# Slot counts of 544, 576 and 600 for the eight experts, and a token's slot computed by bit operations

## The chip, the cores and the metric

The kernel runs on one core of a Trainium2 chip. The metric is the device time of one execution in microseconds (us). The core has a matrix engine (TensorE, PE), a vector engine (VectorE, DVE), a scalar engine (ScalarE, ACT), a general engine (GpSimd, POOL) and a queue engine (SyncE, SP), which run side by side and wait for one another through semaphores. Data moves between the memory of the chip and the on-chip buffers through DMA queues that SP and POOL feed.

## The reference

An attention block feeds a routed two-layer network. Attention has 8 batches, 8 heads, 576 positions and a head width of 64. Scores below the row's maximum less `tau` are dropped before the softmax. The result, rearranged to 4608 tokens of 512 numbers, goes through one of 8 experts, which the token's id alone selects:

```python
expert_idx = token_ids * np.int64(2654435761) % np.int64(E)
out = np.zeros((N, D), dtype=np.float32)
for e in range(E):
    mask = expert_idx == e
    ...
    h = np.maximum(xe @ w1[e], 0.0)      # 512 -> 1024
    out[mask] = h @ w2[e]                # 1024 -> 512
```

All of it is in 32-bit floats. The ids are part of the input; with the reference's inputs the experts get, sorted, 533, 565, 570, 571, 576, 596, 598 and 599 tokens.

## The kernel before, in words

**Attention.** The work is cut into 32 pairs `p` of heads (four pairs of heads, each over eight batches), and each pair into five steps, so that the loop over `n` has 160 steps and a few more to drain. In a step PE forms scores (`score`, L238), DVE negates them and finds the maximum (`negate`, L249), POOL adds the threshold (`thr`, L256), ACT takes the exponential (L263), DVE applies the mask one step later (`mask`, L274), PE turns the weights (L285) and multiplies them with v (L316). Once per pair POOL prepares the denominators (`rec`, L346) and scales the next keys (`scale_k`, L218), and DVE normalises (`put_xm`, L355); SP stores the result to `x_scratch`. The order is written out by hand; each engine works through its instructions in that order.

**Routing.** `route()` (L369 on) is a generator; the attention loop takes one piece of it about twice a pair. It counts the tokens per expert, sorts the experts by count (`pos` is an expert's place in that order, place 0 having the fewest), and gives each token a slot number. Place `e` has `caps[e]` slots for tokens; a token whose rank among its expert's tokens is beyond that goes to overflow tiles, which a loop at the end of the kernel works off (`For_i`, L1138). The table of slots has 608 entries per place, laid out as 32 rows `c` of 19 entries `s`. Entry (c, s) is the token in column 32 s + c of the place's tile: `s` counts squares of 32 columns, `c` the position in a square. With 18 full squares, rank r lies in row r // 18; the kernel computes that by a multiplication with 3641 and a shift, after subtracting what rows of 19 entries hold (`FULL`). After the slot is known (`slot_i`, L526), `scatters()` writes each token's number into one of two tables, one indirect DMA on POOL per step for 36 steps (L551); then SP reads the tables back (L562, L566), and DVE forms the indices for the early gathers (L571, L573).

**Experts.** They are taken by place. Place 0 is started inside the last attention steps: its tokens' rows are gathered by POOL in quarters as the heads finish (`fetch_0`, L122; the last quarter at L831), turned by PE (`early_xT`, L623), and multiplied with three quarters of w1 in `early_h` (L649), pieces of which `fill` puts among the last attention steps; `late_h` (L667) adds the last quarter and takes the ReLU. For the other places both layers are done with seven products of half-size blocks (`seven`, L945) instead of eight, at the cost of block sums on DVE (`sums_w1`, `sums_w2`, `sums_x`, `sums_h`, L862 and L865). The second layer of place 0 is done that way too. A block's width in columns is half of `caps[e]`.

While PE works on the second layer of place `e`, DVE turns the gathered rows of place e + 1 (`turn_x`, L1059), SP moves them into `xT` by sixteen transfers (L1067), and POOL gathers the rows of place e + 2 (`fetch`, L122). For place 1 the gathers start in `late_h`, each behind a small copy (`mark`, L1052) that reads a part of the hidden layer. The output of a place is turned by DVE in two parts (`put_squares`, L1031), and POOL scatters one square of 32 tokens per indirect DMA (L1039). The weights come by SP (L137, L143).

The functions that the diff touches and what calls them, with the profile's line numbers:

Of the kernel before, what the change touches and what calls it, by code (L numbers as in the profile page):

```python
# [9 lines left out]
FP32 = mybir.dt.float32  # L10
# [4 lines left out]
ALU = mybir.AluOpType  # L15
# [5 lines left out]
def kernel(  # L21
# [35 lines left out]
    KT, NB = 5, 19  # L57
    SL = 32 * NB
    CUT = 8
    CAP = SL - CUT  # L60
    FULL = NB * (32 - CUT)
    N_LOW = 5
    LOW = SL - 32
    caps = [LOW] * N_LOW + [CAP] * (E - N_LOW)
# [10 lines left out]
    assert all((r * 3641) >> 16 == r // (NB - 1) for r in range(N))  # L75
# [20 lines left out]
    slot_i = consts.tile([P, NTC], I32, name="slot_i")  # L96
# [50 lines left out]
    with tc.tile_pool(name="a_q", bufs=1) as a_q, \  # L147
# [221 lines left out]
        def route():  # L369
# [10 lines left out]
            cnt = rt_sb.tile([P, 2 * E], FP32, name="cnt")  # L380
# [9 lines left out]
            big = rt_sb.tile([P, NTC], FP32, name="big")  # L390
# [3 lines left out]
            big_e = rt_sb.tile([P, E], FP32, name="big_e")  # L394
# [21 lines left out]
            for e in (0, E // 2):  # L416
# [6 lines left out]
                if e == 0:  # L423
# [22 lines left out]
            nc.gpsimd.tensor_scalar(out=big_e[:], in0=pos[:], scalar1=float(N_LOW),  # L446
                                    scalar2=None, op0=ALU.is_ge)
# [5 lines left out]
                                    op=ALU.mult)  # L453
            yield
            nc.vector.scalar_tensor_tensor(out=key[:], in0=big_e[:], scalar=float(LOW - CAP),
                                           in1=cnt[:, E:2 * E], op0=ALU.mult, op1=ALU.add)
# [3 lines left out]
            nc.vector.tensor_scalar(out=ot_i[:], in0=key[:], scalar1=float(P - 1 - LOW),  # L460
# [14 lines left out]
            nc.vector.scalar_tensor_tensor(out=base[:], in0=pos[:], scalar=float(1 << 19),  # L475
                                           in1=base[:], op0=ALU.mult, op1=ALU.add)
# [14 lines left out]
            nc.vector.tensor_scalar(out=rank_i[:, 2], in0=rank_i[:, 0], scalar1=13, scalar2=63,  # L491
                                    op0=ALU.logical_shift_right, op1=ALU.bitwise_and)
            nc.vector.tensor_scalar(out=rank_i[:, 3], in0=rank_i[:, 0], scalar1=19, scalar2=None,
                                    op0=ALU.logical_shift_right)
            nc.gpsimd.tensor_copy(rank[:], rank_i[:, 1])
            nc.gpsimd.tensor_copy(place[:], rank_i[:, 3])
            nc.gpsimd.tensor_scalar(out=big[:], in0=place[:], scalar1=float(N_LOW),
                                    scalar2=None, op0=ALU.is_ge)
            nc.gpsimd.tensor_copy(ovt[:], rank_i[:, 2])
# [19 lines left out]
            yield  # L519
            nc.gpsimd.tensor_tensor(out=ovt[:], in0=ovt[:], in1=first[:], op=ALU.subtract)  # L520
            yield
            nc.vector.scalar_tensor_tensor(out=ovt[:], in0=rank_f[:], scalar=float(LOW),
                                           in1=ovt[:], op0=ALU.is_gt, op1=ALU.mult)
            nc.gpsimd.tensor_tensor(out=first[:], in0=first[:], in1=rank[:], op=ALU.add)
            yield
            nc.vector.scalar_tensor_tensor(out=slot_i[:], in0=first[:], scalar=-1.0, in1=ovt[:],  # L526
                                           op0=ALU.add, op1=ALU.add)
# [308 lines left out]
    with tc.tile_pool(name="m_x", bufs=1) as m_x, \  # L836
# [4 lines left out]
        NH = LOW // 64  # L841
# [4 lines left out]
        o_q = [m_x.tile([P, n, 32, CO], FP32, name=f"o_q{i}") for i, n in enumerate((NH, NB - NH))]  # L846
# [181 lines left out]
        def put_squares(e, i):  # L1028

            s0, s1 = ((0, NH), (NH, -(-caps[e] // 32)))[i]  # L1030
            nc.vector.transpose(  # L1031
                out=o_q[i][:, 0:s1 - s0].rearrange("p n a c -> p c n a"),
                in_=oT[:, :, 32 * s0:32 * s1].rearrange("p c (n q) -> p c n q", q=32))
# [48 lines left out]
        with tc.manual_schedule():  # L1082
            for e in range(E):
                more = e + 1 < E
# [117 lines left out]
```

## Time and profile before

| | |
|---|---|
| median of 3 runs | 922.66 us (922.28 to 922.70) |
| profiled execution, its own time | 933.93 us |
| its span, first to last instruction | 932.2 us, 20728 instructions |
| TensorE busy | 911.4 us, 98% |
| VectorE busy | 759.5 us, 81% |
| ScalarE busy | 458.3 us, 49% |
| GpSimd busy | 408.1 us, 44% |
| granted TensorE clock | 0.998 |
| DMA | 113.11 MB, mean 121 GB/s |

The profile is that of one execution. Busy shares are averages over stages with different limits, so the tables by stretches and the timeline of a seam say more than the page's first part. A group line gives line, engine, operation, output from input, shapes and count, then the busy time and the mean duration, then the idle time before it and who ended it. "issue" is time in which an engine waited for nothing that the profile shows. Ends of matmuls are modelled, so a PE that is shown busy may still be waiting a little.

### The profile page before, as it was taken

The page shows a single profiled execution, that of the slowest core. Times are in us where ns is not written, and L with a number is a line of the kernel's source. Part 1 is how long each engine was busy: PE and PEld are TensorE (multiplying, and loading weights), DVE is VectorE, ACT ScalarE, POOL GpSimd, SP SyncE. Part 2 cuts the span into 40 slices and gives each one's busy share as a digit, 9 for nine tenths or more (in the row PEclk, how much of TensorE's full clock was granted, in tenths as well). Part 3 has the DMA queues.
Part 4 walks back from the last instruction along what each step waited for, and adds up shares of the span by engine and source line. Part 5 has one row for each costly group of instructions (what it writes and reads, how often), then busy time and mean ns, then how long its engine had stood idle before and what let it go on. Part 6 is the DMA issues. An engine that isn't in the chain of part 4 may idle for free.

```text
span 932.2 us, 20728 instructions
## 1 busy us (share of the span) xinstructions
PE 911.4 (98%) x7495; PEld 662.9 (71%) x7495; DVE 759.5 (81%) x1658; ACT 458.3 (49%) x741; POOL 408.1 (44%) x522
## 2 busy tenths in 40 slices
PE   7999999999999999999999998999999999999996
PEld 4666666666666666665667877888887978879785
DVE  7999999999999999999854685867867686786741
ACT  6888888888888889888702010110202112020210
POOL 4233332436666653465323371643717164350712
PEclk9999999999999999999999999999999999999999
DMA  7355454463555666852113616355352734511101
GB/s 179 88 146 124 107 147 108 120 151 92 115 129 168 151 172 178 211 127 64 32 25 140 191 54 186 126 124 192 93 173 100 196 127 121 200 43 44 46 8 54
DMA packets 114807, 113.11 MB, mean 121 GB/s; under 512 B 32456, under 2 KB 89318, under 8 KB 114704
## 3 DMA queue, kind: packets, MB, share of 16 engines
q1 hardware_dynamic: 105168, 92.64, 37.2%
q0 software_dynamic: 9104, 18.91, 7.2%
q8 instruction: 61, 1.00, 0.4%
q14 instruction: 42, 0.34, 0.1%
q10 hardware_dynamic: 432, 0.21, 0.1%
HBM read 81.99 MB, written 21.50 MB: 111 GB/s over the span
## 4 chain that ended last, share of the span: by engine, by line
PE 62%; issue 21%; POOL 8%; DVE 3%; DMA 2%; ACT 2%; another core or an unknown queue 1%; SPq 1%; POOLq 0%; DVEq 0%; ACTq 0%
PE av L316 18%; PE sc L238 15%; PE bank L945 13%; PE tr L285 11%; POOL out_dram L1039 6%; PE sc L649 3%; PE av L285 1%; POOL xg L122 1%; DMA xT<-xq 1%; ACT w L263 1%; DMA xg<-x_scratch,gidx_x 1%; DMA k_sb<-in_k_dram 1%; ACT wT_b L306 1%; SPq L1067 0%
## 5 line engine op out<-in xcount | busy, mean ns | idle before, releaser
L263 ACT ACTIVATE w<-ns,nmx 128x576 f32<-128x576 f32 x288 | 220.4, 777 | 28.5 <-DVE ns L249 28.2
L1039 POOL DMA_INDIRECT out_dram<-o_q,qidx x128 | 141.0, 1102 | 194.8 <-DVE o_q L1031 133.8
L274 DVE SCALAR_TENSOR_TENSOR w<-ns,thr,w 128x576 f32<-128x576 f32 x288 | 226.2, 817 | 0.0
L249 DVE TENSOR_SCALAR_CACHE_REDUCE ns<-sc 128x576 f32<-128x576 f32 x288 | 205.7, 747 | 7.6 <-PE sc L238 6.6
L256 POOL TENSOR_SCALAR thr<-nmx,drop 128x2 f32<-128x2 f32 (+1 forms) x160 | 104.5, 653 | 186.7 <-DVE ns L249 174.1
L238 PE MATMUL sc<-k_sb,q 64*128 64x288 f32 (+1 forms) x1280 | 178.6, 423 | 0.9 <-DVE ns L249 0.5
L285 PEld LDWEIGHTS tr<-ident,w 64*128 64x128 f32 x2624 | 106.1, 138 | 94.6 <-ACT wT_b L306 32.7
L285 PE MATMUL tr<-ident,w 64*128 64x64 f32 x2624 | 139.0, 230 | 6.1 <-ACT wT_b L306 2.8
L952 ACT ACTIVATE h<-h 128x576 f32<-128x576 f32 (+1 forms) x56 | 38.8, 693 | 158.8 <-DVE h L865 127.8
L238 PEld LDWEIGHTS sc<-k_sb,q 64*128 64x128 f32 (+1 forms) x1280 | 92.8, 177 | 23.2 <-DVE ns L249 8.5
L955 ACT COPY p<-bank 128x576 f32<-128x576 f32 (+2 forms) x22 | 14.0, 635 | 183.4 <-PE bank L945 157.9
L316 PE MATMUL av<-wT_a,v 128*64 128x320 f32 (+1 forms) x704 | 100.4, 418 | 0.4 <-DVE xm L355 0.3
L945 PE MATMUL bank<-h,w_sb 128*128 128x288 f32 (+2 forms) x384 | 95.6, 405 | 2.3 <-issue 1.5
L945 PEld LDWEIGHTS bank<-h,w_sb 128*128 128x128 f32 x384 | 92.5, 294 | 4.2 <-issue 1.9
L306 ACT COPY wT_a<-tr 128x512 f32<-128x512 f32 (+1 forms) x128 | 81.7, 638 | 20.7 <-PE tr L285 20.2
L306 ACT COPY wT_b<-tr 128x512 f32<-128x512 f32 (+1 forms) x128 | 81.4, 636 | 15.3 <-PE tr L285 8.6
L945 PE MATMUL bank<-xT,w_sb 128*128 128x288 f32 (+1 forms) x336 | 87.5, 410 | 0.0
L316 PE MATMUL av<-wT_b,v 128*64 128x256 f32 x640 | 83.2, 389 | 0.0
L945 PEld LDWEIGHTS bank<-xT,w_sb 128*128 128x128 f32 x336 | 63.8, 190 | 19.0
L945 PE MATMUL bank<-h_s,w_s 128*128 128x288 f32 (+2 forms) x256 | 63.0, 404 | 1.9 <-DVE h_s L862 1.9
L316 PEld LDWEIGHTS av<-wT_a,v 128*64 128x64 f32 x704 | 43.7, 136 | 29.2 <-DVE xm L355 0.8
L945 PEld LDWEIGHTS bank<-h_s,w_s 128*128 128x128 f32 x256 | 50.0, 195 | 13.3 <-DVE h_s L862 2.3
(168 smaller groups left out, 1117.7 us busy)
## 6 DMA issues: line engine op xcount, KB each, us to landing
w_sb<-in_moe_w_dram SPq DMA_DIRECT2D x16, 2048.0 KB
q<-in_q_dram SPq DMA_DIRECT2D x62, 288.0 KB
v<-in_v_dram SPq DMA_DIRECT2D x32, 256.0 KB
x_scratch<-xm SPq DMA_DIRECT2D x32, 256.0 KB
xT<-xq SPq DMA_DIRECT2D x84, 80.0 KB
k_sb<-in_k_dram SPq DMA_DIRECT2D x31, 144.0 KB
k_sb<-in_k_dram SPq DMA_DIRECT2D x32, 112.0 KB
x_scratch<-xg SPq DMA_DIRECT2D x9, 256.0 KB
```

Of the source, the lines that this page charges most:

```text
L238: nc.tensor.matmul(sc[out_rows, i, 0:S2], lhsT=q_sb[rows, h, q0:q1], rhs=k_sb[rows, h], start=True, stop=True)
L249: nc.vector.tensor_scalar(out=ns[:].rearrange("p (i s) -> p i s", i=2), in0=sc[:, :, 0:S2], scalar1=-1.0, scalar2=None, op0=ALU.mult, op1= ...
L256: nc.gpsimd.tensor_scalar(out=thr[:, 0:j + 1], in0=stats[n][0][:, 0:j + 1], scalar1=drop[:], scalar2=None, op0=ALU.add)
L263: nc.scalar.activation(w, nss[n, j][:], AF.Exp, bias=stats[n][0][:, j:j + 1], scale=-1.0)
L274: nc.vector.scalar_tensor_tensor(out=w, in0=nss.pop((n, j))[:], scalar=stats[n][1][:, j:j + 1], in1=w, op0=ALU.is_le, op1=ALU.mult, accum_ ...
L285: nc.tensor.transpose(dst[:, r, 64 * c:64 * c + 64], src[rows, c0:c0 + P], ident[rows, rows])
L306: nc.scalar.copy(dst, tr[:, :, 0:64 * n_c].rearrange("p r (c q) -> p r c q", c=n_c))
L316: nc.tensor.matmul(av[64 * j:64 * j + 64, g, c0:c1], lhsT=v_sb[:, c, 64 * j:64 * j + 64], rhs=wT[g][:, i, c0:c1], start=(c == 0), stop=stop)
L649: nc.tensor.matmul(h_ps[:, i, 0:CH0], lhsT=w1_sb[:, co, fo * P:fo * P + P], rhs=xT_0[:, co, i * CH0:i * CH0 + CH0], start=(co == 0), stop= ...
L945: nc.tensor.matmul(ps[:, i, 0:width], lhsT=lhsT, rhs=y[:, c], start=c == 0, stop=c == n_k - 1)
L952: nc.scalar.activation(c, c, AF.Relu)
L1039: inst = nc.gpsimd.indirect_dma_start(out=rows[:, :], out_offset=bass.IndirectOffsetOnAxis(ap=idx, axis=0), in_=o_sb, in_offset=None, boun ...
```

## The change

Place 0 gets 544 slots, places 1 to 4 get 576 and places 5 to 7 get 600; before, places 0 to 4 had 576 and the others 600. A token's rank `r` is now its column: it lies in square r >> 5, at position r & 31, so its slot is 608 e + 19 (r & 31) + (r >> 5). Before, neighbours in rank lay in neighbouring squares at the same position. The steps between the three slot counts are applied on POOL by comparing the place with 1 and with 5. Four DVE instructions fewer form the slot, eight POOL instructions more do, and `route()` has three pieces fewer before the slots are known. In `put_squares` the first part of a place has `caps[e] // 64` squares, 8 for place 0 and 9 for the others; before it was 9 for all.

```diff
-    FULL = NB * (32 - CUT)
-    N_LOW = 5
-    LOW = SL - 32
-    caps = [LOW] * N_LOW + [CAP] * (E - N_LOW)
+    STEPS = ((1, 32), (5, 24))
+    LOW = CAP - sum(d for _, d in STEPS)
+    caps = [LOW + sum(d for e0, d in STEPS if e >= e0) for e in range(E)]
...
-            nc.gpsimd.tensor_scalar(out=big_e[:], in0=pos[:], scalar1=float(N_LOW),
-                                    scalar2=None, op0=ALU.is_ge)
...
-            nc.vector.scalar_tensor_tensor(out=key[:], in0=big_e[:], scalar=float(LOW - CAP),
-                                           in1=cnt[:, E:2 * E], op0=ALU.mult, op1=ALU.add)
+            for e0, d in STEPS:
+                nc.gpsimd.tensor_scalar(out=more_e[:], in0=pos[:], scalar1=float(e0),
+                                        scalar2=float(-d), op0=ALU.is_ge, op1=ALU.mult)
+                nc.gpsimd.tensor_tensor(out=cnt[:, E:2 * E], in0=cnt[:, E:2 * E], in1=more_e[:],
+                                        op=ALU.add)
+            nc.gpsimd.tensor_scalar(out=pos[:], in0=pos[:], scalar1=float(1 << 19), scalar2=-1.0,
+                                    op0=ALU.mult, op1=ALU.add)
...
-            nc.vector.scalar_tensor_tensor(out=base[:], in0=pos[:], scalar=float(1 << 19),
-                                           in1=base[:], op0=ALU.mult, op1=ALU.add)
+            nc.gpsimd.tensor_tensor(out=base[:], in0=base[:], in1=pos[:], op=ALU.add)
...
-            nc.gpsimd.tensor_scalar(out=big[:], in0=place[:], scalar1=float(N_LOW),
-                                    scalar2=None, op0=ALU.is_ge)
...
+            for e0, d in STEPS:
+                nc.gpsimd.tensor_scalar(out=more[:], in0=place[:], scalar1=float(e0),
+                                        scalar2=float(-d), op0=ALU.is_ge, op1=ALU.mult)
+                nc.gpsimd.tensor_tensor(out=rank[:], in0=rank[:], in1=more[:], op=ALU.add)
+            yield
+            nc.vector.tensor_scalar(out=rank_i[:, 2], in0=rank_i[:, 1], scalar1=5, scalar2=None,
                                     op0=ALU.logical_shift_right)
...
-            nc.vector.scalar_tensor_tensor(out=rank_f[:], in0=big[:], scalar=float(-FULL),
-                                           in1=rank[:], op0=ALU.mult, op1=ALU.add)
-            nc.gpsimd.tensor_scalar(out=rank_f[:], in0=rank_f[:], scalar1=-1.0, scalar2=0.0,
-                                    op0=ALU.add, op1=ALU.max)
...
-            yield
-            nc.vector.tensor_scalar(out=rank_i[:, 0], in0=rank_f[:], scalar1=3641.0, scalar2=None,
-                                    op0=ALU.mult)
-            nc.vector.tensor_scalar(out=rank_i[:, 0], in0=rank_i[:, 0], scalar1=16, scalar2=None,
-                                    op0=ALU.logical_shift_right)
+            nc.vector.tensor_scalar(out=rank_i[:, 3], in0=rank_i[:, 1], scalar1=31, scalar2=None,
+                                    op0=ALU.bitwise_and)
...
             nc.vector.scalar_tensor_tensor(out=first[:], in0=place[:], scalar=float(SL),
-                                           in1=rank_i[:, 0], op0=ALU.mult, op1=ALU.add)
-            nc.vector.scalar_tensor_tensor(out=rank_f[:], in0=big[:], scalar=float(LOW - CAP),
-                                           in1=rank[:], op0=ALU.mult, op1=ALU.add)
-            nc.vector.scalar_tensor_tensor(out=ovt[:], in0=big[:], scalar=float(LOW - CAP),
-                                           in1=ovt[:], op0=ALU.mult, op1=ALU.add)
-            yield
+                                           in1=rank_i[:, 2], op0=ALU.mult, op1=ALU.add)
+            nc.vector.scalar_tensor_tensor(out=first[:], in0=rank_i[:, 3], scalar=float(NB),
+                                           in1=first[:], op0=ALU.mult, op1=ALU.add)
...
-            nc.vector.scalar_tensor_tensor(out=slot_i[:], in0=first[:], scalar=-1.0, in1=ovt[:],
-                                           op0=ALU.add, op1=ALU.add)
+            nc.vector.scalar_tensor_tensor(out=ovt[:], in0=rank[:], scalar=float(LOW),
+                                           in1=ovt[:], op0=ALU.is_ge, op1=ALU.mult)
+            nc.vector.tensor_tensor(out=slot_i[:], in0=first[:], in1=ovt[:], op=ALU.add)
...
-            s0, s1 = ((0, NH), (NH, -(-caps[e] // 32)))[i]
+            n_half = caps[e] // 64
+            s0, s1 = ((0, n_half), (n_half, -(-caps[e] // 32)))[i]
```

More of the change, by code (lines that the diff above doesn't have):

```diff
@@ L74 @@
                for m in range(1, E + 1) if m * (LOW + 1) <= N)
-    assert all((r * 3641) >> 16 == r // (NB - 1) for r in range(N))
     slot_dram = [nc.dram_tensor(f"slot_scratch_{i}", (NSLOT, 1), I32, kind="Internal").ap()
@@ L389, in route @@
             ovt = rt_sb.tile([P, NTC], FP32, name="ovt")
-            big = rt_sb.tile([P, NTC], FP32, name="big")
+            more = rt_sb.tile([P, NTC], FP32, name="more")
             place = rt_sb.tile([P, NTC], FP32, name="place")
@@ L393, in route @@
             pos = rt_sb.tile([P, E], FP32, name="pos")
-            big_e = rt_sb.tile([P, E], FP32, name="big_e")
+            more_e = rt_sb.tile([P, E], FP32, name="more_e")
             order = rt_sb.tile([P, E], FP32, name="order")
@@ L459, in route @@
             yield
-            nc.vector.tensor_scalar(out=ot_i[:], in0=key[:], scalar1=float(P - 1 - LOW),
+            nc.vector.tensor_scalar(out=ot_i[:], in0=cnt[:, E:2 * E], scalar1=float(P - 1 - LOW),
                                     scalar2=float(P - 1), op0=ALU.add, op1=ALU.max)
@@ L490, in route @@
                                     scalar2=None, op0=ALU.bitwise_and)
-            nc.vector.tensor_scalar(out=rank_i[:, 2], in0=rank_i[:, 0], scalar1=13, scalar2=63,
+            nc.vector.tensor_scalar(out=rank_i[:, 2], in0=rank_i[:, 0], scalar1=19, scalar2=None,
+                                    op0=ALU.logical_shift_right)
+            nc.vector.tensor_scalar(out=rank_i[:, 3], in0=rank_i[:, 0], scalar1=13, scalar2=63,
                                     op0=ALU.logical_shift_right, op1=ALU.bitwise_and)
-            nc.vector.tensor_scalar(out=rank_i[:, 3], in0=rank_i[:, 0], scalar1=19, scalar2=None,
-                                    op0=ALU.logical_shift_right)
@@ L495, in route @@
-            nc.gpsimd.tensor_copy(rank[:], rank_i[:, 1])
-            nc.gpsimd.tensor_copy(place[:], rank_i[:, 3])
-            nc.gpsimd.tensor_scalar(out=big[:], in0=place[:], scalar1=float(N_LOW),
-                                    scalar2=None, op0=ALU.is_ge)
-            nc.gpsimd.tensor_copy(ovt[:], rank_i[:, 2])
-            yield
-            nc.vector.scalar_tensor_tensor(out=rank_f[:], in0=big[:], scalar=float(-FULL),
-                                           in1=rank[:], op0=ALU.mult, op1=ALU.add)
@@ L503, in route @@
-            nc.gpsimd.tensor_scalar(out=rank_f[:], in0=rank_f[:], scalar1=-1.0, scalar2=0.0,
-                                    op0=ALU.add, op1=ALU.max)
+            nc.gpsimd.tensor_copy(rank[:], rank_i[:, 1])
+            nc.gpsimd.tensor_copy(place[:], rank_i[:, 2])
+            nc.gpsimd.tensor_copy(ovt[:], rank_i[:, 3])
+            for e0, d in STEPS:
+                nc.gpsimd.tensor_scalar(out=more[:], in0=place[:], scalar1=float(e0),
+                                        scalar2=float(-d), op0=ALU.is_ge, op1=ALU.mult)
+                nc.gpsimd.tensor_tensor(out=rank[:], in0=rank[:], in1=more[:], op=ALU.add)
@@ L508, in route @@
-            nc.vector.tensor_scalar(out=rank_i[:, 0], in0=rank_f[:], scalar1=3641.0, scalar2=None,
-                                    op0=ALU.mult)
-            nc.vector.tensor_scalar(out=rank_i[:, 0], in0=rank_i[:, 0], scalar1=16, scalar2=None,
-                                    op0=ALU.logical_shift_right)
+            nc.gpsimd.tensor_tensor(out=ovt[:], in0=ovt[:], in1=rank[:], op=ALU.add)
             yield
             nc.vector.scalar_tensor_tensor(out=first[:], in0=place[:], scalar=float(SL),
-                                           in1=rank_i[:, 0], op0=ALU.mult, op1=ALU.add)
@@ L515, in route @@
-            nc.vector.scalar_tensor_tensor(out=rank_f[:], in0=big[:], scalar=float(LOW - CAP),
-                                           in1=rank[:], op0=ALU.mult, op1=ALU.add)
-            nc.vector.scalar_tensor_tensor(out=ovt[:], in0=big[:], scalar=float(LOW - CAP),
-                                           in1=ovt[:], op0=ALU.mult, op1=ALU.add)
-            yield
+                                           in1=rank_i[:, 2], op0=ALU.mult, op1=ALU.add)
+            nc.vector.scalar_tensor_tensor(out=first[:], in0=rank_i[:, 3], scalar=float(NB),
+                                           in1=first[:], op0=ALU.mult, op1=ALU.add)
@@ L520, in route @@
             nc.gpsimd.tensor_tensor(out=ovt[:], in0=ovt[:], in1=first[:], op=ALU.subtract)
             yield
[L522 to L525, printed above, removed]
-            nc.vector.scalar_tensor_tensor(out=slot_i[:], in0=first[:], scalar=-1.0, in1=ovt[:],
-                                           op0=ALU.add, op1=ALU.add)
+            nc.vector.scalar_tensor_tensor(out=ovt[:], in0=rank[:], scalar=float(LOW),
+                                           in1=ovt[:], op0=ALU.is_ge, op1=ALU.mult)
@@ L840 @@
         F2, C2, FH, D2, NG = F // 2, CO // 2, FO // 2, DIN // 2, FO // 4
-        NH = LOW // 64
         out_q = out.rearrange("n (g m) -> (n g) m", g=4)
@@ L845 @@
         oT = m_x.tile([P, CO, SL], FP32, name="oT")
-        o_q = [m_x.tile([P, n, 32, CO], FP32, name=f"o_q{i}") for i, n in enumerate((NH, NB - NH))]
+        o_q = [m_x.tile([P, n, 32, CO], FP32, name=f"o_q{i}") for i, n in enumerate((CAP // 64, NB - CAP // 64))]
         nc.gpsimd.memset(oT[:, :, CAP:SL], 0.0)
```

## The prediction

> **What bounds the kernel now.** I read the page's first part, then the table by stretches, and then the timeline wherever TensorE had a gap. The page: TensorE is busy 98% of the span. The table by stretches (busy time of PE, PEld, DVE, ACT, POOL, then clock, DMA share, GB/s) shows two regimes: attention up to about 465 us with PE and DVE both full, and the experts after it with PE full and DVE at two thirds.
>
> ```profile
> PE 911.4 (98%) x7495; PEld 662.9 (71%) x7495; DVE 759.5 (81%) x1658; ACT 458.3 (49%) x741; POOL 408.1 (44%) x522
> ...
> 100.00:200.00 100.00, 99.82 (x1218) 61.68 (x1218) 99.29 (x291) 85.96 (x140) 34.47 (x66) 1.00 0.50 124
> ...
> 600.00:640.00 40.00, 40.00 (x166) 34.92 (x165) 29.53 (x37) 5.84 (x9) 14.50 (x14) 1.00 0.46 127
> ```
>
> The change touches two places: routing, inside attention, and the first expert (place 0, the smallest count), from about 459 to 534 us. What a narrower matmul is worth I take from the groups with shapes kept apart (count | busy us, mean ns | idle before). Each matmul of the code leaves two records.
>
> ```profile
> L945 PE MATMUL bank<-h,w_sb 128*128 128x300 f32 x96 | 24.9, 416 | 0.0
> ...
> L945 PE MATMUL bank<-h,w_sb 128*128 128x240 f32 x48 | 10.0, 366 | 0.0
> ```
>
> 60 columns are 50 ns, 0.833 ns a column; 300 against 288 columns (416, 406 ns) gives the same. So 16 columns fewer (272 for 288) are 13.3 ns a record.
>
> Then the timeline (start, us, what, idle before) at the seams of place 0: the last x store and its gathers, and the first sums of the second expert.
>
> ```profile
> 480.30 1.10 POOL L122 DMA_INDIRECT xg<-x_scratch,gidx  x1 [6.04 <-DMA x_scratch<-xm]
> ...
> 486.73 1.45 POOL L122 DMA_INDIRECT xg<-x_scratch,gidx  x1 [0.30 <-issue]
> ...
> 491.28 0.39 PEld L623 LDWEIGHTS tr<-ident,xg 64*128 64x128 f32 x9 [0.39 <-issue]
> ...
> 528.91 0.76 DVE L862 TENSOR_TENSOR x_s<-xT 128x576 f32<-128x576 f32 x1 [5.42 <-DMA xT<-xq]
> ...
> 530.38 2.25 DVE L1031 STREAM_TRANSPOSE o_q<-oT 128x1152 f32<-128x1152 f32 x1
> ...
> 534.70 4.12 PE L945 MATMUL bank<-x_s,w_s 128*128 128x288 f32 x16 [0.36 <-DVE x_s L862]
> ...
> 570.81 7.07 PE L945 MATMUL bank<-h_s,w_s 128*128 128x288 f32 x28 [1.86 <-DVE h_s L862]
> ```
>
> At 491.28 PE does not wait for the gathers; they land under the matmuls of L649. At 534.70 it does wait, for sums of an x that arrived by DMA at 528.91. The chain of waits shows where that x comes from:
>
> ```profile
> 505.16 6.33 DMA xg<-x_scratch,gidx_x
> ...
> 511.84 3.08 DVE xq L1059 x5
> 514.92 0.02 SPq L1067
> ...
> 526.89 2.00 DMA xT<-xq
> 528.89 0.02 issue
> 528.91 0.77 DVE x_s L862
> ```
>
> That is gather, turn on DVE, sixteen SP transfers, sums: none of it gets shorter by narrowing place 0. The 570.81 line is the end of a jam, below.
>
> **What the skill says.** "TensorE: Matmul & The Clock Gate", "Part 2: What happens when you issue a matmul": one column of the moving operand enters per cycle, so time goes with columns. The trace agrees in kind; its 0.833 ns is two cycles of the page's 2.4 GHz, and I use the measured slope. "VectorE: DVE Perf Modes", "The TRN2 errata": a fixed cost per instruction dominates small operands. Agrees: 128x8 takes 0.16 us and 128x36 0.18 to 0.19, so the number of DVE instructions counts. "DMA: Bandwidth & Descriptors", "Anatomy of one DMA": about 2 us fixed, most of it the write receipt. The last x store leaves SP by 478.3 and POOL goes on at 480.30: 2.0. "Runtime: NRT & Kernel Launch", "Instruction fetch mechanics": each sequencer fetches its instructions in 16 KiB blocks through its own DMA queue. The page's queue table has such a queue (q8 instruction, 61 packets, 1.00 MB: 16 KB each).
>
> **The change, part by part.**
>
> *No overflow either way.* The counts of this input, sorted, are 533, 565, 570, 571, 576, 596, 598, 599; before they fit 576 x 5 and 600 x 3, after they fit 544, 576 x 4, 600 x 3. The overflow loop stays empty. Only place 0 changes its size.
>
> *Routing on DVE.* Out: L455 0.16, L475 0.17, and eight from L501 to L526, 1.49; in: two bit operations 0.17 each, two for `first` 0.19 each, two at the end 0.19 and 0.18, 1.09. Net -0.73 us. How much of DVE time shows: the POOL additions of L346 mark pairs; they start at 35.47 and 77.30 (three pairs, 13.94 each) and at 77.30 and 220.11 (ten pairs, 14.28 each). So 3.4 us for routing whose DVE instructions in that stretch sum to 6.3: about 0.54. That gives -0.4.
>
> *Routing on POOL.* 10 instructions become 18, some 0.3 us each (L503 0.35, L524 0.26): +2.4 us of an engine that is 35% busy. The dangerous one is the piece at 175 us: four more instructions behind the casts (L499 ends at 176.8) push the `rec` additions (177.59), `scale_k` and then `thr` (178.96), which stand back to back, by 0.1 to 0.4 us. `thr` ends at 179.76 and DVE's mask that uses it starts at 180.94, so 1.2 us cover it; without cover it is 0.4 us once. The piece at 103 us adds five, done by about 105.6, before `rec` at 106.09. I charge 0.2 for port and queue effects (bounds 0 to 0.8). Attention together: -0.2.
>
> *Slots found three pieces sooner.* `placed` comes in the step at 193.8 instead of 210.7, so the 36 scatters (1.3 us each on POOL) and the sixteen table reads on SP (350.8 to 363.3 now, then about 17 us sooner) move up. The scatters stay one a step. The reads then leave SP ahead of the second w1 load instead of behind it; DVE takes sidx now at 369.5, well after, and gidx_0 is needed after 380. Cost 0, covered by about 10 us of distance.
>
> *Rank order.* A gather's row p now holds neighbours in rank rather than every 18th. Descriptors and bytes are the same; no trace here shows what the order does to memory. Bounded -0.5 to +1.5, taken 0.
>
> *Place 0's matmuls.* early_h 48 products (96 records), late_h 16 (32), layer2 56 (112). In order of time:
> 1. Of early_h, 24 records run between 462.8 and 474 amid the last attention work, with DVE mostly idle: 24 x 13.3 = -0.32. The last x store and the gathers move with it.
> 2. The 64 records from 475.56: -0.85. The page's 2 us after the last gather's issue (488.2) gives an estimated landing at 490.2; moved, 489.9, and PE would arrive at 491.28 - 1.17 = 490.1. Just covered; the last gather has also 21 valid rows instead of some 60.
> 3. Eight more, and late_h up to the mark that releases the gathers of the second expert (20 records): -0.37. So that chain starts about 1.6 sooner (with DVE's narrower adds, 0.04 each).
> 4. layer2: 112 x 13.3 = 1.49 for PE. But PE now meets the x_s wait: its third product is ready at 533.9 less 3.2 in all, while x_s comes 1.6 sooner by the chain. On DVE in front of it, `put_squares` turns 8 squares instead of 9 (2.25/9 = 0.25) and three adds are 0.04 shorter: 0.37. So of 1.49 only about 0.4 passes, and PE's gap at 534.7 grows from 0.4 to about 1.5 us. DVE is full from 529 to 550, so nothing makes this up afterwards.
>
> One scatter fewer of place 0 (L1039, 1.3 us with its gap) is off the path: POOL.
>
> *Sum* for the profiled execution (933.93 us, span 932.2): -0.2 - 0.32 - 0.85 - 0.37 - 0.05 - 0.4 = -2.2, so 931.7, span 930.0. The median 922.66 lies 11.3 under the profiled one; I carry the difference over: **920.5**. What a measurement of this kernel can tell from no change is about 0.2%, 1.85 us, so this stands just past it.
>
> **Rivals.**
>
> *A. All 240 records pass* (the x chain moves as far as PE, or the sums have slack): 240 x 13.3 = 3.2, with attention 919.3. For: DVE's add at 511.16 in front of the turns is PE-driven and moves 2.1. Against: the chain's DMA piece ends at 511.49. 0.05.
>
> *B. The last gather is exposed.* If it lands at 490.9 now, hidden by luck, step 2 gives 0.3 instead of 0.85 or less: 921.3. For: the gap may be tight. Against: fewer rows in it. 0.15.
>
> *C. The jam eases.* Between 557.8 and 577.5 PE runs 64 records that take 15.5 elsewhere (7.75 for 32): 4.15 lost. PE and DVE stop together and resume at 566.86 and 566.90, PE put down to "issue", DVE to an unknown queue, with DMA share at 1.0; by the runtime page an instruction fetch behind data fits. The five gathers there stand behind the scatters of place 0 on POOL (last at 556.95); one fewer lets them start 1.3 us earlier against the moves. At the next experts, where the gathers lead the moves by 2 to 4 us, PE loses nothing. If it vanishes: 916.4. Against: two engines' fetches also depend on where blocks end. 0.20.
>
> *D. Slower: the jam grows.* Same place, other sign: x chain and gathers no longer start with the same distance to PE, so another fetch is caught. It outweighs the gain once it costs more than 6.4 instead of 4.15, and by 0.2% from 8.2; doubled, 924.6. The 570.81 line speaks for it being sensitive; the quiet experts after it against. 0.18, with a slow rank order counted here.
>
> **How the numbers follow.** The likeliest, 0.42, is 920.5, own range 919.5 to 921.5; about 0.30 of it faster by over 0.2%, 0.12 within. A 0.05 faster; C 0.20 faster; B 0.15: 0.02 faster, 0.13 within; D 0.18 slower. Faster 0.57, within 0.25, slower 0.18. The range 916.4 to 924.2 leaves out the ends of C and D.
>
> **What would show it.** Matmuls of L649, L667 and the first layer2 at 272 columns, about 393 ns. PE's gap before the first product with x_s near 1.5 us, put down to DVE x_s or to the DMA xT<-xq (A: under 0.5). The first transposes of L623 in the last batch with no wait for xg (B: a wait). Pairs between 77 and 220 at 14.2 to 14.3. The 64 records of the second layer2 in 15.5 (C), 19.6, or 24 (D). It is wrong if attention moves by over 0.7, or the jam changes by over 1.5.

## The result, and the profile after

The changed kernel takes 920.07 us (median of 13 runs, 919.22 to 921.47); the kernel before takes 922.70 us beside it (13 runs, 922.02 to 923.83). The ratio is 0.9973, 95% interval 0.9965 to 0.9980, or 2.6 us less with 1.8 to 3.2 as its bounds. The prediction was 920.5.

The profiled execution of the changed kernel took 920.07 us, its span is 918.5. The profile of before that the prediction read took 933.93 us, 11 above its kernel's median. Two more profiles of it were taken; the one called *before_third* (923.27 us, span 921.7) is 0.57 above the median, and what follows compares with that one. One set of four runs (before_again, after_again, old_sizes, wide_layer2) fell on an occasion when every kernel, the one before too, took some 20 us longer; it is compared only within itself.

The page of the kernel after, its first part, and below it two lines of the table by stretches (busy time of PE, PEld, DVE, ACT, POOL with their counts, then clock, DMA share, GB/s):

```profile
PE 905.0 (99%) x7495; PEld 661.7 (72%) x7495; DVE 757.1 (82%) x1654; ACT 457.2 (50%) x741; POOL 410.4 (45%) x528
...
100.00:200.00 100.00, 99.66 (x1216) 61.39 (x1212) 99.38 (x289) 85.91 (x140) 39.08 (x76) 1.00 0.50 124
600.00:640.00 40.00, 40.00 (x166) 35.00 (x165) 27.47 (x32) 3.61 (x6) 13.08 (x13) 1.00 0.57 177
```

The regimes are as before: DVE and PE both full in attention, PE alone after it. POOL has ten instructions more between 100 and 200 us; DVE is as full as before.

The groups by shape show the narrower products of place 0 (count | busy us, mean ns | idle before):

```profile
L641 PE MATMUL sc<-xT,w_sb 128*128 128x272 f32 x96 | 24.4, 402 | 0.0
...
L936 PE MATMUL bank<-h,w_sb 128*128 128x272 f32 x48 | 11.8, 402 | 0.8 <-DVE h L664 0.8
```

And the timeline of after at the same seams of place 0 (start, us, what, idle before): the gathers behind the last x store, the transposes of the last batch, and the first sums of the second expert.

```profile
473.19 1.10 POOL L120 DMA_INDIRECT xg<-x_scratch,gidx  x1 [5.94 <-DMA x_scratch<-xm]
...
479.55 1.42 POOL L120 DMA_INDIRECT xg<-x_scratch,gidx  x1 [0.30 <-issue]
...
483.59 0.53 PEld L615 LDWEIGHTS tr<-ident,xg 64*128 64x128 f32 x9 [0.36 <-issue]
...
519.12 0.76 DVE L853 TENSOR_TENSOR x_s<-xT 128x576 f32<-128x576 f32 x1 [4.61 <-DMA xT<-xq]
519.91 0.76 DVE L853 TENSOR_TENSOR xT<-xT 128x576 f32<-128x576 f32 x1
520.59 2.01 DVE L1023 STREAM_TRANSPOSE o_q<-oT 128x1024 f32<-128x1024 f32 x1
...
524.88 4.04 PE L936 MATMUL bank<-x_s,w_s 128*128 128x288 f32 x16
```

At 483.59 PE still waits for no gather. The line to look at is the last one: no bracket. Before, PE waited here for the sums of the second expert, and the prediction let this wait grow to about 1.5 us; it is gone.

**Where the time went, by stretches.** The marks are the starts of POOL's `rec` (the one near 35 us, the one near 206, the last near 456), of the 64 unbroken `early_h` records, of layer 2 of place 0, of layer 1 of place 1, and of its first product with `x_s`. Each number is the difference of two starts in one kernel's timeline, in us; the last row is what remains of the span, given to a tenth, so that the rows of a column add up to it.

| stretch | before | after | old sizes | one step | spread | 536 slots | both |
|---|---|---|---|---|---|---|---|
| to the mark near 35 | 35.35 | 35.27 | 35.01 | 35.39 | 35.45 | 34.91 | 35.45 |
| routing, to 206 | 170.41 | 170.74 | 170.62 | 170.25 | 170.25 | 170.26 | 170.25 |
| attention, to 456 | 250.15 | 249.65 | 249.65 | 249.70 | 249.48 | 249.64 | 249.67 |
| to the 64 records | 13.02 | 12.84 | 13.01 | 13.02 | 12.84 | 12.76 | 12.76 |
| to layer 2 | 27.33 | 26.31 | 27.35 | 27.34 | 26.31 | 26.02 | 26.03 |
| layer 2 of place 0 | 27.39 | 26.19 | 27.38 | 27.39 | 26.19 | 26.02 | 26.03 |
| to the first `x_s` product | 4.47 | 3.88 | 4.10 | 3.88 | 4.73 | 4.79 | 5.21 |
| the rest | 393.58 | 393.62 | 393.58 | 393.53 | 393.65 | 393.50 | 393.70 |
| span | 921.7 | 918.5 | 920.7 | 920.5 | 918.9 | 917.9 | 919.1 |

Before is before_third; the five columns after "after" are the kernels of the experiments old_sizes_b, one_step, spread, place0_536 and spread_536. Between before and after: routing +0.33, the attention after it -0.50, the two `early_h` and `late_h` stretches -0.18 and -1.02, layer 2 -1.20, the wait for `x_s` -0.59.

### The profile page after: what moved, and what is told of

Read it like the earlier page. It is cut to its first block, busy times and chain, and to the rows that moved or that the text cites. A ratio compares the mean times of both kernels' runs of the same rounds, so it can differ in the third digit from the quotient of the medians.

```text
span 918.5 us, 20725 instructions
## 1 busy us (share of the span) xinstructions
PE 905.0 (99%) x7495; PEld 661.7 (72%) x7495; DVE 757.1 (82%) x1654; ACT 457.2 (50%) x741; POOL 410.4 (45%) x528
## 4 chain that ended last, share of the span: by engine, by line
PE 71%; issue 16%; POOL 5%; DMA 3%; DVE 2%; ACT 2%; SPq 0%; POOLq 0%; DVEq 0%; ACTq 0%
PE bank L936 23%; PE av L314 18%; PE sc L236 15%; PE tr L283 10%; POOL out_dram L1031 4%; PE sc L641 3%; DMA out_dram<-o_q,qidx 2%; PE av L283 1%; DVE ns L247 1%; POOL xg L120 1%; DVE w L272 1%; ACT w L261 1%; DMA k_sb<-in_k_dram 1%; PE xT_ps L659 0%; PE sc L659 0%
## 5 line engine op out<-in xcount | busy, mean ns | idle before, releaser
L1031 POOL DMA_INDIRECT out_dram<-o_q,qidx x127 | 139.0, 1094 | 189.4 <-DVE o_q L1023 151.6
L283 PEld LDWEIGHTS tr<-ident,w 64*128 64x128 f32 x2624 | 106.2, 138 | 88.1 <-ACT wT_b L304 25.8
L946 ACT COPY p<-bank 128x576 f32<-128x576 f32 (+3 forms) x22 | 14.0, 636 | 193.4 <-PE bank L936 193.4
L936 PE MATMUL bank<-h,w_sb 128*128 128x288 f32 (+3 forms) x384 | 94.6, 403 | 0.8 <-DVE h L664 0.8
L936 PE MATMUL bank<-h_s,w_s 128*128 128x288 f32 (+3 forms) x256 | 62.3, 402 | 0.0
```

What stands on the lines that cost most here:

```text
L283: nc.tensor.transpose(dst[:, r, 64 * c:64 * c + 64], src[rows, c0:c0 + P], ident[rows, rows])
L936: nc.tensor.matmul(ps[:, i, 0:width], lhsT=lhsT, rhs=y[:, c], start=c == 0, stop=c == n_k - 1)
L1031: inst = nc.gpsimd.indirect_dma_start(out=rows[:, :], out_offset=bass.IndirectOffsetOnAxis(ap=idx, axis=0), in_=o_sb, in_offset=None, boun ...
```

## The experiments

**Before, twice more, and after once more.** The kernels as they are.

> The kernel before, once more, for a second profiled execution. If the stop of both engines at 565 us and the short stops in attention belong to the kernel, they stand at the same places and the profiled time is again near 934. If they belong to that one execution (the median is 922.7), the profiled time is 922 to 924, the 64 records of the second expert's layer2 take 15.5 us and not 19.6, and attention pairs take 13.9 instead of 14.1 to 14.5.

> The changed kernel unedited, in the same rounds as the two next ones, so that they can be compared with it: 920.1 give or take 0.5.

> The kernel before in a third profiled execution. The two so far stop at 565 us for 4 us and wait 0.4 us for x_s. If both belong to the kernel they are there again. If they come only in executions near 935 us, then an execution near 922 us shows neither; then what the widths bring there is the narrower matmuls alone, about 2.4 us by the traces so far (0.22 + 1.03 + 1.19).

before_again took 939.14 us (span 937.5) and has the jam that the prediction saw in the second expert's layer 2; the timeline there:

```profile
565.27 0.40 PE L945 MATMUL bank<-h,w_sb 128*128 128x288 f32 x1 [0.39 <-issue]
566.18 0.62 PE L945 MATMUL bank<-h,w_sb 128*128 128x288 f32 x1 [0.50 <-issue]
567.59 1.38 PE L945 MATMUL bank<-h,w_sb 128*128 128x288 f32 x5 [0.79 <-issue]
...
571.55 7.06 PE L945 MATMUL bank<-h_s,w_s 128*128 128x288 f32 x28 [1.62 <-DVE h_s L862]
```

before_third has none of it: the same 64 records, `bank<-h,w_sb` and `bank<-h_s,w_s`, take 15.52 us (551.48 to 567.00):

```profile
551.48 7.92 PE L945 MATMUL bank<-h,w_sb 128*128 128x288 f32 x32
559.24 7.92 PE L945 MATMUL bank<-h_s,w_s 128*128 128x288 f32 x32
567.00 1.38 PE L945 MATMUL bank<-h_s,w_sb 128*128 128x288 f32 x5
```

The changed kernel has none in its profile (548.15 to 563.67, 15.52 too), but in after_again they take 17.89. So whether there is a jam goes with the occasion. Its size may depend on the change: in that one set it is 19.79 and 19.86 us with 576 slots for place 0 (before_again, old_sizes), 17.89 and 17.43 with 544 (after_again, wide_layer2). With one profile each, this is not shown. after_again took 938.84 us, ratio 0.9959 [0.9941, 0.9977], beside a before at 942.26: the gain is there in that set as well.

**Old sizes (old_sizes, old_sizes_b).** All of the new routing and rank order, but 576 slots for place 0.

```diff
-    STEPS = ((1, 32), (5, 24))
+    STEPS = ((1, 0), (5, 24))
```

> The changed kernel with the first step of the slot counts set from 32 to 0, so places 0 to 4 have 576 again: the new way to a slot and the new order of tokens with the old widths. If the widths are the whole gain, this is 922.5, -0.2 against before (routing alone, as predicted). If the new rank order or the routing carries part of it, it is 921.5 or less. If the rank order costs something that the widths hide, it is 923.2 or more.

> The new routing and rank order with the old sizes (576 slots for places 0 to 4, 600 for three), against the kernel before. Theory 'widths': nearly all of the gain belongs to place 0's columns; what is left is +0.3 us in the routing (pair mark 2 to the mark near 206 in 170.7 us instead of 170.4) and -0.5 us between there and the last mark: ratio 0.9990 to 1.0000, some 922.3 us where the kernel before takes 922.7. Rival 'shift': the wait of PE for the second expert's sums also goes with the new routing, as it did with one step and the old sizes (0.43 us less): ratio 0.9988 or less, some 921.6 us. The wait before the first product with x_s in the trace tells them apart: 0.3 to 0.5 us in the first case, none in the second.

944.26 us, ratio 0.9997 [0.9975, 1.0020], and the second time 922.42 us, ratio 0.9995 [0.9987, 1.0004]. Without the narrower place 0 no gain can be told from nothing, and the interval of the second run does not meet that of the changed kernel: the gain comes with the smaller place 0, and the new rank order as such costs nothing that shows. The stretches agree. The three of place 0 are those of before to 0.02 us, the attention behind the routing is shorter by 0.50, as it is by 0.45 to 0.67 in every kernel with the new order, and the routing is 0.21 longer. The wait for `x_s` did not settle anything: 4.10 us, between the two values that the theories named.

**One step, old sizes (one_step).** As above, with one pass fewer through each of the two loops over the steps, four POOL instructions.

```diff
-    STEPS = ((1, 32), (5, 24))
+    STEPS = ((5, 24),)
```

> The changed kernel with the old widths (576 for places 0 to 4) and only one step between slot counts, so four GpSimd instructions fewer than old_sizes: two in the piece at 103 us, two in that at 175. Theory: these instructions push the scaling of the next keys (scale_k) under DVE's mask, which reads two tensors from SBUF, and the mask then takes 1.1 to 1.3 us instead of 0.81. With four fewer, the mask after each of the two pieces takes 0.81 again, and the second to the fourteenth rec stand 0.3 to 0.5 us closer. Rival: it is the added work itself that slows DVE; then about half of the loss stays.

922.06 us, span 920.5. The routing takes 170.25 us, less than before's 170.41, and PE does not wait for `x_s` (3.88). So the +0.33 of the routing comes with the two loops' second pass on POOL, and the wait can go away without one column being taken out. It is one execution.

**Layer 2 of place 0 at its old width (wide_layer2, wide_layer2_b).** Zero columns fill the hidden layer of place 0 up to 576, so that layer 2 runs at 288 columns a product and everything ahead of it at 272. Nothing is left out.

```diff
+            nc.gpsimd.memset(h_0[:, :, caps[0]:576], 0.0)
...
-            return caps[e] // 2 if e < E - 1 else CHL
+            return 288 if e == 0 else caps[e] // 2 if e < E - 1 else CHL
```

> The changed kernel, but layer2 of the first expert works on 576 columns again (the 32 added columns of its input are zeros written early by GpSimd), early_h and late_h on 544. By the prediction only 0.4 of layer2's 1.49 us passes, because the next expert's x comes late: +0.4 over the changed kernel, 920.5, and TensorE waits less at the first product with x_s. If x is there in time (rival A), all of it passes: +1.5, 921.6.

> layer2 of place 0 on 576 columns once more, to halve the uncertainty. By the trace of the changed kernel, layer2 is 1.2 us shorter there than before (25.96 against 27.15) and TensorE never waits for x_s, so if the prediction's step 4 (0.4 passes) is wrong, this is 1.2 above the changed kernel; if it is right, 0.4.

938.92 us, ratio 0.9963 [0.9946, 0.9981], and 920.85 us, ratio 0.9978 [0.9971, 0.9984]. In the trace of the second, layer 2 takes 27.38 us again, and the first product with `x_s` follows after 3.88: the whole 1.19 comes back, and no wait takes any of it. That trace is against the prediction's step 4, which let only 0.4 of layer 2 reach the end. The times do not decide between 0.4 and 1.2: by the medians the cost is 0.8 (920.85 against 920.07, from two sets, the ratios' intervals overlapping), and 0.1 in the first set.

**A third step (fit).** Sizes 536, 568, 576 x 3, 600 x 3.

```diff
-    STEPS = ((1, 32), (5, 24))
+    STEPS = ((1, 32), (2, 8), (5, 24))
...
-        nc.gpsimd.memset(oT[:, :, CAP:SL], 0.0)
+        nc.gpsimd.memset(oT[:, :, LOW:SL], 0.0)
```

> 536 slots for place 0 (533 tokens) and 568 for place 1 (565), by a third step; GpSimd clears 64 columns of the output buffer instead of 8. If time goes with columns, place 0 gives 240 x 8 x 0.83 = 1.6 us and place 1 its 224 records the same, 1.5: 3.1 below the changed kernel, less 0.2 to 0.6 for four more GpSimd instructions. If the strided weights of layer2 hold a record at 233 ns, place 0 gives only 1.2 and the sum is 2.7, less the same.

919.80 us, ratio 0.9966 [0.9952, 0.9980], span 918.3. The routing takes 171.01 us, 0.60 more than before: the third pass costs about what the second did, but not by a longer mask. Both masks take 0.81 or 0.82 us there. POOL's `rec` now comes behind their start, takes 1.14 and 1.12 us for its two additions instead of 0.55, and DVE waits 0.43 us for it twice (107.96 and 179.60). PE waits 0.95 us for `x_s` by the timeline, where spread, below, has 0.69. The smaller sizes win about as much as these two lose. The expectation was missed, and in part for a slip of its own: eight slots fewer are four columns fewer in a product of half-size blocks, so that its 3.1 us should have been about half of that. Against after, place 0's three rows gave 0.54 and the last row, with most of place 1, another 0.6.

**The loops one piece later (spread).** The same instructions; each of the two loops over the steps stands one `yield` later, behind `order_i` and behind the two bit operations.

```diff
-            for e0, d in STEPS:
-                nc.gpsimd.tensor_scalar(out=more[:], in0=place[:], ...)
-                nc.gpsimd.tensor_tensor(out=rank[:], in0=rank[:], in1=more[:], op=ALU.add)
             yield
             nc.vector.tensor_scalar(out=rank_i[:, 2], in0=rank_i[:, 1], scalar1=5, ...)
             nc.vector.tensor_scalar(out=rank_i[:, 3], in0=rank_i[:, 1], scalar1=31, ...)
+            for e0, d in STEPS:
+                nc.gpsimd.tensor_scalar(out=more[:], in0=place[:], ...)
+                nc.gpsimd.tensor_tensor(out=rank[:], in0=rank[:], in1=more[:], op=ALU.add)
```

> The changed kernel, with the two loops over the steps moved one piece of the routing later, away from the denominators and the key scaling of the same pair on POOL; no instruction more or fewer. Theory 'ports': the key scaling on POOL, pushed 0.4 us later by those loops, runs beside DVE's mask and stretches it (1.10 and 1.32 us instead of 0.81), which is the +0.33 us of the routing. Then both masks take 0.81 again, pair mark 2 to the mark near 206 takes 170.2 to 170.4 us instead of 170.74, and the kernel is 0.3 to 0.5 us faster than the changed one: ratio to before 0.9967 against 0.9972. Rival 'sum of POOL': what counts is the eight instructions more on POOL, wherever they stand: the stretch stays at 170.7 and the time at that of the changed kernel.

919.84 us, ratio 0.9967 [0.9955, 0.9980]. First the routing. In the timeline of after, the loop ends at 177.76, the denominators stand right behind it and the key scaling behind those:

```profile
177.82 0.55 POOL L344 TENSOR_SCALAR rec<-rs 128x9 f32<-128x9 f32 x2
...
178.47 0.75 POOL L216 TENSOR_SCALAR k_sb<-k_sb,k_scale 128x576 f32<-128x576 f32 x1
...
178.50 1.32 DVE L272 SCALAR_TENSOR_TENSOR w<-ns,thr,w 128x576 f32<-128x576 f32 x1
```

In the timeline of spread the scaling comes 0.55 us ahead of the mask, and the mask takes its usual 0.81:

```profile
177.99 0.75 POOL L216 TENSOR_SCALAR k_sb<-k_sb,k_scale 128x576 f32<-128x576 f32 x1
...
178.54 0.81 DVE L272 SCALAR_TENSOR_TENSOR w<-ns,thr,w 128x576 f32<-128x576 f32 x1
```

The other stretched mask in after's routing, 1.10 us at 107.12, is at 0.81 too, and the routing takes 170.25 instead of 170.74. With no POOL instruction more or fewer, the theory of the ports held here against that of the sum of POOL. What it would be worth at the end did not show: the whole kernel is not told apart from after, and some 0.5 us could not be with an interval 2.3 us wide. In the profile the wait for `x_s` came back, 0.85 us by the table. The chain of waits of spread at that seam is the chain of before again. It runs through SP's sixteen transfers, while the chain of after stays on PE from 494.81 to beyond the first `x_s` product. Spread:

```profile
506.08 0.73 SPq L1059
...
508.16 6.98 DMA xT<-xq
...
515.15 0.58 SPq L1059
...
517.72 2.00 DMA xT<-xq
519.72 0.02 issue
519.74 0.77 DVE x_s L853
...
521.29 1.97 DVE o_q L1023
```

Before (before_third), the same pieces:

```profile
508.33 0.73 SPq L1067
...
510.40 7.34 DMA xT<-xq
...
517.75 0.58 SPq L1067
...
520.32 2.00 DMA xT<-xq
522.32 0.02 issue
522.34 0.77 DVE x_s L862
...
523.89 2.18 DVE o_q L1031
```

SP issues eleven of the sixteen transfers, and the twelfth waits until the fourth has landed: 7.34 us in before, 6.98 in spread. That wait is the program's: in the traces the sixteen use eight semaphores in turn, and the twelfth waits on the one that the fourth raises when it lands. From SP's first transfer to DVE's first sum it is 14.01 us in before, 13.66 in spread and 12.56 in after (506.56 to 519.12).

**536 slots for place 0 (place0_536), and both (spread_536).**

```diff
-    STEPS = ((1, 32), (5, 24))
+    STEPS = ((1, 40), (5, 24))
...
-        nc.gpsimd.memset(oT[:, :, CAP:SL], 0.0)
+        nc.gpsimd.memset(oT[:, :, LOW:SL], 0.0)
```

> The changed kernel with 536 slots for place 0 (sizes 536, 576 x 4, 600 x 3; the smallest count is 533). Theory 'floor': 4 columns fewer a product are worth 3.3 ns a record where the weights are dense: early_h and late_h 128 x 3.3 = -0.4 us, layer2 about 56 x 3.3 = -0.2, nothing for the layer2 records whose weights are dealt with a stride (233.75 ns at 272 and at 268 columns). So -0.6 us against the changed kernel, ratio 0.9966, about 919.5 us, if PE's wait for x_s stays away; with that wait back at 0.9 us, as in the kernel with three steps, +0.3 us: 920.4. Rival 'columns': all 240 records go by columns, -0.8 us, and layer2 of place 0 takes 25.8 us instead of 26.2.

> The two together: the loops over the steps one piece later, and 536 slots for place 0. If 'ports' and 'floor' hold and the two do not meet, -0.4 and -0.6 us against the changed kernel: ratio to before 0.9962, about 919.2 us. If the wait for x_s comes back (0.9 us), 920.0. If neither holds, it is at the changed kernel's ratio, 0.9972.

919.36 us, ratio 0.9961 [0.9948, 0.9975], and 919.97 us, ratio 0.9970 [0.9959, 0.9981]. Neither is told apart from the changed kernel; 536 slots has the lowest median of all that ran, in five runs. Layer 2 takes 26.02 us, not 25.8: the floor, not the columns. The timeline of after, PE, in layer 2 of place 0:

```profile
494.81 7.86 PE L936 MATMUL bank<-h,w_sb 128*128 128x272 f32 x32 [0.81 <-DVE h L664]
502.51 7.50 PE L936 MATMUL bank<-h_s,w_s 128*128 128x272 f32 x32
509.84 3.90 PE L936 MATMUL bank<-h_s,w_sb 128*128 128x272 f32 x16
513.58 3.91 PE L936 MATMUL bank<-h,w_sb 128*128 128x272 f32 x16
517.33 3.83 PE L936 MATMUL bank<-h,w_s 128*128 128x272 f32 x16
```

and that of the kernel with 536 slots:

```profile
493.59 7.86 PE L936 MATMUL bank<-h,w_sb 128*128 128x268 f32 x32 [0.81 <-DVE h L664]
501.29 7.39 PE L936 MATMUL bank<-h_s,w_s 128*128 128x268 f32 x32
508.51 3.90 PE L936 MATMUL bank<-h_s,w_sb 128*128 128x268 f32 x16
512.25 3.91 PE L936 MATMUL bank<-h,w_sb 128*128 128x268 f32 x16
516.00 3.78 PE L936 MATMUL bank<-h,w_s 128*128 128x268 f32 x16
```

From start to start, the blocks with `w_sb` take 7.70, 3.74 and 3.74 or 3.75 us in both, 234 ns a record behind the first block, at 272 and at 268 columns. The blocks with `w_s` go by columns, 7.33 against 7.22.

The routing has a surprise: 170.26 us without spreading. The order on POOL is that of after, yet no mask is stretched. In its timeline the mask is first by 0.32 us, and the key scaling is the one that is stretched, from 0.75 to 1.10:

```profile
178.01 0.81 DVE L272 SCALAR_TENSOR_TENSOR w<-ns,thr,w 128x576 f32<-128x576 f32 x1
...
178.33 1.10 POOL L216 TENSOR_SCALAR k_sb<-k_sb,k_scale 128x576 f32<-128x576 f32 x1
```

So in the order of after it is a matter of some tenths of a microsecond which of the two is late. The same goes for the pair near 107: there the mask is stretched in after and wide_layer2_b, while in after_again, the two runs of old sizes, wide_layer2 and this kernel the mask is first by about 0.1 us and the scaling takes 1.33 or 1.34. With the loops moved the routing took 170.25 in both kernels that had them moved.

## Why the prediction was right, and where it was not

The sum was -2.2 us; the profiles differ by -3.2, the medians by -2.6. That the sum came this near is luck in part, since two of its errors have opposite signs: up to layer 2 the columns gave 0.4 less than it had (-1.20 for -1.59), layer 2 and the wait behind it 1.4 more (-1.79 for -0.4). Point by point:

**The columns.** The slope of 13.3 ns a record for 16 columns was right where PE streams without a wait: the 48 records of layer 2 with `w_s` went from 11.64 to 11.00 us, -0.64 for 48 x 13.3 = 0.64. Step 1 gave -0.18 instead of -0.32; its cause was not followed up. From the 64 records up to layer 2 there are 104 (64, eight more, 32 of `late_h`), by the slope -1.39; measured is -1.02: the 64 went from 15.72 to 15.10 us, -0.62 for 0.85, and the rest from 11.61 to 11.21, -0.40 for 0.53. In the 64, the wait of the weight loads on DVE's additions `h` went from 0.2 us to 0.4, which about covers what is missing there; a faster PE meets DVE.

**Layer 2 has a floor that the prediction did not have.** It took 112 x 13.3 = 1.49 for PE's part; the part measured 1.20. The missing 0.3 lies in the 64 records with `w_sb`. Before (before_third, PE's blocks, then the weight loads of layer 2):

```profile
504.25 7.92 PE L945 MATMUL bank<-h_s,w_s 128*128 128x288 f32 x32
512.01 4.04 PE L945 MATMUL bank<-h_s,w_sb 128*128 128x288 f32 x16
515.89 4.04 PE L945 MATMUL bank<-h,w_sb 128*128 128x288 f32 x16
...
L945 PEld LDWEIGHTS bank<-h,w_sb 128*128 128x128 f32 x48 | 11.8, 309 | 1.3 <-DVE h L672 1.3
L945 PEld LDWEIGHTS bank<-h_s,w_s 128*128 128x128 f32 x32 | 6.3, 196 | 1.4
```

and the loads after:

```profile
L936 PEld LDWEIGHTS bank<-h,w_sb 128*128 128x128 f32 x48 | 11.4, 317 | 1.2 <-DVE h L664 1.2
L936 PEld LDWEIGHTS bank<-h_s,w_s 128*128 128x128 f32 x32 | 6.3, 196 | 1.0
```

From start to start, all blocks stood 242.5 ns a record apart before (7.76 us for 32, 3.88 for 16). The slope of 0.833 ns a column makes 229 of it at 272 columns. That is what the blocks with `w_s` have; those with `w_sb` have 234. The slope itself was sound: the 240-column records of the last expert stand 202.5 ns apart (879.67 to 886.15 for 32 in after), which is the same 0.833. But `w2_blocks` deals the weights of the other experts only, that is, takes for a product every fourth column of them (every second one of their sums), so that the group of 240 columns could not show what dealt weights do. The Trainium skill, "TensorE: Matmul & The Clock Gate", "Part 2: What happens when you issue a matmul", says that the next tile's weights load while this tile's product runs. The traces agree, and show where that cover may end: the weight loads of `w_sb` in layer 2, whose elements stand four apart, take 309 ns at 288 columns and 317 at 272, those of `w_s`, two apart, 196 and 196, and those of `early_h` and of the last expert, side by side, 190. Only the first kind kept the spacing up, at 234 ns for 272 and for 268 columns, while the last expert's weights, under the same names but not dealt, let it fall to 202.5. That the load is what holds it is inferred from this; no run gave the weights of place 0 another layout. The mean duration of a group says little here: 402 ns stands at both lines shown at 272 columns, though only one of the two has the floor.

**Step 4 was wrong in size: it took SP's transfers as fixed.** The prediction had PE's arrival 3.2 us sooner and `x_s` about 2.0 (1.6 by the chain, 0.37 on DVE), so that PE would wait about 1.5. (Its 533.9 for PE's readiness does not go with the gap of 0.36 before 534.70, which gives 534.34; the 1.5 comes from the gap.) Measured, SP's first transfer came 1.77 sooner (508.33, 506.56), and the way from DVE's first sum to the first product shrank by 0.27 (5.78 in before, 5.51 in spread, where PE waits; `o_q` 2.18 to 1.97 in the chains). Both are near the predicted 1.6 and 0.37. But the sixteen transfers took 12.56 us instead of 14.01, and that is the 1.45 which the prediction had not. Most of it, 1.19, lies between the issue of the eleventh and of the twelfth (2.37 us before, 1.18 after): the fourth, for which the twelfth waits, had landed sooner. With 519.12 + 5.51 = 524.63 the sums are ready 0.25 ahead of PE at 524.88. Had the transfers kept their 14.01, the sums would come at 526.08 and PE would wait 1.2 us (worked out, not run); the kernels where they take long show such waits by the table's row, over the 3.88 without one: 0.85 in spread (13.66), 0.91 with 536 slots (13.59), 1.33 with both (14.01). The way in which PE's wait comes about was right; the transfers' length was the term that failed.

**What sets the transfers' length is open.** It is much the same for repeats of one kernel: 13.94, 14.04 and 14.01 in three profiles of before, 12.56 and 12.43 in two of after, 13.84 and 13.63 with old sizes, 12.83 and 11.97 with the wide layer 2. It differs between kernels that are alike there: after and spread issue the same work from 206 us on, and one_step (12.34) has the columns of before. Nor do the columns decide it: it is short in one_step and in wide_layer2_b (11.97), long in spread. The transfers share the DMA engines with five gathers for the third expert, which in after start 2.17 us ahead of SP's first (504.39), and in spread as well (503.91, 506.08), so their distance is no answer either. One rival is left: the four profiles of the last set (old_sizes_b, spread, 536 slots, both) are all long, and the changed kernel was not profiled in that set. That old sizes were long in another set too, and that in each of two other sets long and short stand side by side, speaks against it but does not exclude it.

**Attention: right by errors that cancel.** The prediction gave -0.2: -0.4 for DVE instructions, +0.2 for POOL. Measured -0.17, but as +0.33 in the routing and -0.50 after it. In the four kernels of the table in which no mask of the routing was longer by over 0.1 us (one step, spread, 536 slots, both) it takes 170.25 or 170.26 us, 0.16 less than before; with the 0.15 gained between 206 and 220 us, where the last piece of the routing used to stand, the estimate for DVE is -0.31. The stretched masks of after cost 0.49 against those four. POOL's "port and queue effects" were the right suspect with too small a size, inside the bounds of 0.8. The piece at 175 us was the right place; the wrong step was to ask only whether `thr` would come late. It is the key scaling that meets the mask, and the mask, on full DVE, pays. The piece at 103 us was put at nothing, "done by about 105.6"; in after its last instruction ended at 106.16, and `rec` and the scaling came late there as well. The other 0.35 of the -0.50 lies in the last pair, where before PE waited 0.34 for `xm` at 454.40. Why that wait went was not traced.

**The rivals.** A, all 240 records pass: near the truth in its end, and the x chain did move as far as PE (DVE's first sum from 522.34 to 519.12), but through shorter transfers, which A did not name; the floor took 0.3 of it. B, a gather exposed: no wait for xg at 483.59. C and D, the jam: the 64 records at 15.5 us, the sign that was to speak for C, did come, but the runs took the ground from both, since a profile of before near its median has no jam either. On the occasion with a jam it was about 2 us shorter with the narrower place 0, as said above, so that C is open for such occasions. The ends of the predicted range were set by these two, from a jam that the prediction had in one profile only.

## What to carry to other kernels

Price a narrower matmul by the spacing of its records from start to start, and take the slope from products whose weights lie as those do: here one with strided weights stopped at 234 ns where the others went on falling. Before a stage is called bound by a chain of transfers, compare the chain's length in more than one kernel or profile: here it varied by 2 us, as much as the whole change. And an engine with room to spare is not free to take work: a few tenths of delay on POOL put a 0.75 us instruction beside one on full DVE that needs the same port.

## What was not expected of the hardware

POOL's key scaling and DVE's mask, both 128x576 with their operands in SBUF, keep each other waiting, and the one that starts first goes through at its usual time: DVE 1.32 us instead of 0.81 when the scaling started 0.03 us earlier, POOL 1.10 instead of 0.75 when the mask started 0.32 us earlier. The Trainium skill, "SBUF — State Buffer", "Who interferes with whom", says that a DVE instruction with two SBUF inputs contends with a GpSimd instruction that reads SBUF, and that the order of issue decides who blocks. The traces agree on who waits, and show how long: the mask at 178.50 was lengthened by 0.51 us where the scaling had 0.72 still to run, the one at 107.12 by 0.29 where it had 0.50 (106.87 and 0.75), one at 207.08 by 0.11 where it had 0.32 (206.65 and 0.75), and that of spread at 178.54 not at all where it had 0.20. So about the last 0.2 us of the scaling's span held nobody up. DVE's negation, which the key scaling ran beside in before, kept its 0.75 us there; its input is in PSUM.

The jam, in which PE and DVE stop together with no release on record, came with the occasion: of the second expert's layer 2, the first 64 records take 15.52 us at 288 columns in every profile near 920 us, of before, of after and of the variants, and 17.4 to 19.9 in the five above 930, the lower two with 544 slots for place 0. What stops the two engines there is open.
